# Moving small halo copies and two value loads from SyncE's queue to GpSimd's, in a convolution and gated-MLP gradient kernel

## The chip, the cores and the metric

The kernel runs on one core of a Trainium2 chip. The metric is the device time of one execution in microseconds, as the median of several runs. A core has five engines with a program each: TensorE (PE in the profile; its weight loads are PEld), VectorE (DVE), ScalarE (ACT), GpSimd (POOL) and SyncE (SP). Each works through its own program in order and waits on semaphores. A DMA transfer is started by an instruction of one of the engines; in this kernel SyncE and GpSimd start nearly all, and the page lists SyncE's as queue q1 (hardware_dynamic) and GpSimd's as q0 (software_dynamic). The transfers themselves run on the core's 16 DMA engines.

## The reference

The inputs are bfloat16, with S = 2048 rows, D = 512 columns and F = 1376. The forward function has two branches on the layer-normalised input `xn`:

```python
xn = layernorm(q)
# branch A: short convolution of k over 4 rows, product with v, long convolution
k_shift = sum(k_pad[:, t:t+S, :] * shift_k[:, 3 - t] for t in range(4))   # k_pad: 3 rows of zeros ahead
kv = k_shift * v
y  = irfft(rfft(pad(kv)) * rfft(pad(ssm_k)))[:S] + kv * ssm_D
s  = xn * y
# branch B: gated MLP
h  = sigmoid(xn @ w_gate) * (xn @ w_up)
out = q + s * silu(h @ w_down)
```

The kernel returns `out` and the gradients of a vector-Jacobian product with `grad_out`: of q, k, v, shift_k, ssm_k, ssm_D and of the three weight matrices. So it holds the forward long convolution, the MLP with its backward pass, the long convolution backward, and the short convolution backward. In the latter, `dks = dkv * v` and then `dk[row] = sum over lag 0..3 of dks[row + lag] * shift_k[lag]`.

## The kernel before

Rows are laid out as `row = 16 * partition + j`, so a partition holds 16 rows that follow each other. The 512 columns are treated in NG = 4 groups of GW = 128. A short convolution needs, beside the 16 rows of a partition, the three rows of its neighbour: the halo. In the forward stage a group of k is loaded with three extra rows in front:

```python
def ld_halo(eng, dst, src):
    eng.dma_start(dst[1:113], src[0:112])
    eng.dma_start(dst[113:128], src[112:127])

def ld_k(cp):
    c0, c1 = cp * GW, (cp + 1) * GW
    kh = kh_r.next()                                     # two buffers
    nc.gpsimd.memset(kh[0:1, 0:3, :], 0.0)
    nc.sync.dma_start(kh[:, 3:, :], kC[:, :, c0:c1])     # 16 rows, 512 KB
    ld_halo(nc.sync, kh[:, 0:3, :], kHalo[:, 0:3, c0:c1])   # 84 KB and 11.2 KB
    stA["kh", cp] = kh

def ld_v(cp):
    vg = vg_r.next()                                     # two buffers
    nc.sync.dma_start(vg, vC[:, :, cp * GW:(cp + 1) * GW])
    stA["vg", cp] = vg

def strV():                                              # VectorE part of branch A
    for cg in range(NG):
        # ... acc = short convolution of kh over four lags, 128x2048 each
        nc.gpsimd.dma_start(ksh_d[cg], acc.rearrange("p j d -> p (j d)"))   # shifted k, for the backward stage
        nc.vector.tensor_tensor(kvt, acc, vg, ALU.mult)
        if cg + 2 < NG:
            ld_k(cg + 2)
            ld_v(cg + 2)
        # ... first step of the transform of kvt
```

The K spectra of the same stage are stored with `nc.gpsimd.dma_start(KK_d[cg, qq, 0], KF)`, and their two halves are swapped by two copies of SyncE, `Ks[0:64] <- KF[64:128]` and `Ks[64:128] <- KF[0:64]`. The MLP's `h` is stored by GpSimd in `hF_d`.

In the backward stage, a group multiplies by the stored spectra `KK` (loaded by SyncE, three buffers), goes through the inverse steps `inv3` and `inv1` on TensorE with PSUM evictions on ScalarE or VectorE, and ends with the short convolution backward on VectorE:

```python
nc.vector.tensor_tensor(dks[:, 0:NJ, :], dkv, vg, ALU.mult)
nc.vector.memset(dks[96:P, NJ:NJ + 3, :], 0.0)
nc.sync.dma_start(dks[0:112, NJ:NJ + 3, :], dks[1:113, 0:3, :])      # halo from the next partition
nc.sync.dma_start(dks[112:127, NJ:NJ + 3, :], dks[113:128, 0:3, :])
nc.vector.tensor_tensor(dkv, dkv, ksh, ALU.mult)
# ... gradient of ssm_k: 32 matmuls, 2 evictions, 512 KB out
# ... gradient of shift_k: 64 matmuls of 32 columns (the diagonal), a product and a reduction on VectorE
for lag in range(4):
    src = dks[:, lag:lag + NJ, :]                        # lags 1 to 3 read the halo
    # lag 0: dk = src * skl;  lags 1 to 3: term = src * skl; dk = dk + term
# ... every second group: nc.sync.dma_start(o2C[...], dk)   (1 MB)
```

TensorE fills its time in this stage with the weight gradients `dW`: 35 blocks of 16 matmuls with 512 or 352 columns, each followed by an eviction and a store by SyncE. They depend on nothing in the backward convolution.

The order of instructions is not the order of this text. All operations are recorded first, with the regions that they read and write (the columns of a buffer, not its partitions, so the second halo copy of `dks` waits for the first). Then a list scheduler with a model of each engine, and of one pipe of transfers for GpSimd and one for the others, fixes the order of every engine, which engine does an eviction, and the PSUM banks:

```python
pipe = {"gpsimd": 0.0, "hw": 0.0}
# ...
if op.dma:
    occ, d = self.dcost(alt)
    me, other = ("gpsimd", "hw") if e == "gpsimd" else ("hw", "gpsimd")
    # ... start after this pipe's earlier transfers; fin = end of the transfer + a constant
```

All instructions are emitted from one line of the scheduler, L522, so the profile is read by operation and shape, not by line.

Of the kernel before, what the change touches and what calls it, by code (L numbers as in the profile page):

```python
# [23 lines left out]
NJ = 16  # L24
# [3 lines left out]
GW = D // NG  # L28
# [603 lines left out]
def cview(ap3):  # L632
    return ap3[0].rearrange("(p j) d -> p j d", j=NJ)
# [3 lines left out]
def kernel_impl(ctx, tc, A_q, A_k, A_v, A_shift_k, A_ssm_k, A_ssm_D, B_x, B_w_gate, B_w_up, B_w_down,  # L637
                grad_out, out_0, out_1, out_2, out_3, out_4, out_5, out_6, out_7, out_8, out_9):
    nc = tc.nc
    qC, kC, vC, goC = cview(A_q), cview(A_k), cview(A_v), cview(grad_out)  # L640
    o0C, o1C, o2C, o3C = cview(out_0), cview(out_1), cview(out_2), cview(out_3)
    kHalo = A_k[0][13:13 + 16 * 127].rearrange("(p j) d -> p j d", j=16)
# [15 lines left out]
    def ps_mm(shape, dt=f32, name=None):  # L658
        return nc.ps(PS["mm"], shape, dt)
# [142 lines left out]
# [5 lines that stand above are left out]
        c0, c1 = cp * GW, (cp + 1) * GW  # L807
        kh = kh_r.next()
        nc.gpsimd.memset(kh[0:1, 0:3, :], 0.0)
        nc.sync.dma_start(kh[:, 3:, :], kC[:, :, c0:c1])  # L810
        ld_halo(nc.sync, kh[:, 0:3, :], kHalo[:, 0:3, c0:c1])
        stA["kh", cp] = kh

    def ld_v(cp):
        vg = vg_r.next()
        nc.sync.dma_start(vg, vC[:, :, cp * GW:(cp + 1) * GW])
        stA["vg", cp] = vg

    skr_r = Ring(ar, [D * 4])
# [123 lines left out]
    def step3T(Qf, rows, qq, dst, sw):  # L943
        if rows:
            ps = ps_mm([64, 8, 2], name="ps_x")
            for h in range(2):
                src = Qf.rearrange("p (k g) -> p k g", g=64)[:, 32 * h:32 * h + 32, 16 * qq:16 * qq + 16]
                nc.tensor.matmul(ps[:, 32 * h:32 * h + 32].rearrange("p k g x -> p k (g x)"), BDq, src, start=True, stop=True)
            pv = ps.rearrange("p k g x -> p g k x")
            v = lambda a: a.rearrange("p (g k x) -> p g k x", g=8, x=2)  # L950
        else:
            pv = ps = ps_mm([1024], name="ps_x")
            for h in range(2):
                o = 1024 * qq + 512 * h
                nc.tensor.matmul(ps[:, h * 512:(h + 1) * 512], BDq, Qf[:, o:o + 512], start=True, stop=True)
            v = lambda a: a
        nc.evac(v(dst), pv[:], 1024)
        nc.scalar.copy(v(sw[0:64]), pv[64:128])
        nc.scalar.mul(v(sw[64:128]), pv[0:64], -1.0)
# [349 lines left out]
    def ld_KK(n):  # L1309
        if n < 16:  # L1310
            KK = KK_r.next()
            nc.sync.dma_start(KK, KK_d[n // 4, n % 4].rearrange("t p x -> p t x"))
            stC["KK", n] = KK
# [10 lines left out]
    def ld_bwd(cg):  # L1324
        c0, c1 = cg * GW, (cg + 1) * GW
        if cg % 2 == 0:
            stC["vg"] = vg_r.next()
            nc.sync.dma_start(stC["vg"], vC[:, :, c0:c0 + 256])
        ksh, kh = ksh_r.next(), kh_r.next()
        nc.sync.dma_start(ksh.rearrange("p j d -> p (j d)"), ksh_d[cg])  # L1330
        nc.gpsimd.memset(kh[0:1, 0:3, :], 0.0)
        nc.sync.dma_start(kh[:, 3:, :], kC[:, :, c0:c1])
        ld_halo(nc.sync, kh[:, 0:3, :], kHalo[:, 0:3, c0:c1])
        stC["bwd", cg] = (ksh, kh)

    def backC():
        for cg in range(NG):
            c0, c1 = cg * GW, (cg + 1) * GW
            B1, B2 = B1_r.next(), B2_r.next()
            ys = {}  # L1340
            for qq in range(5):
                if qq < 4:
                    n = cg * 4 + qq
                    while ("Qf", cg) not in stC:
                        yield 0
                    Xc, Xw = Xc_r.next(), Xw_r.next()
                    step3T(stC["Qf", cg], cg > 1, qq, Xc, Xw)
                    stC["nY"] = n + 1
                    yield 1024
                    KK = stC.pop(("KK", n))  # L1350
                    PP = P_r.next()
                    for t in range(2):
                        nc.vector.tensor_tensor(PP[:, t], Xc, KK[:, t], ALU.mult)
                        nc.vector.tensor_tensor(KK[:, t], Xw, KK[:, t], ALU.mult)
                    ys[qq] = (PP, KK)
                if qq == 2:
                    ld_bwd(cg)
                if qq > 0:
                    PP, KK = ys.pop(qq - 1)
                    inv3([(PP[:, 0], RC1), (KK[:, 0], RS2)], qq - 1, B1)  # L1360
                    yield 2048
                    inv3([(PP[:, 1], RC1), (KK[:, 1], RS2)], qq - 1, B2, True)
                    ld_KK(cg * 4 + qq + 2)
                    yield 2048
            dkv = y2A[:, :, c0:c1]
            yield from inv1(B1, dkv)
            ksh, kh = stC.pop(("bwd", cg))
            vg = stC["vg"][:, :, (cg % 2) * GW:(cg % 2 + 1) * GW]
            dks = dks_r.next()
            nc.vector.tensor_tensor(dks[:, 0:NJ, :], dkv, vg, ALU.mult)  # L1370
            nc.vector.memset(dks[96:P, NJ:NJ + 3, :], 0.0)
            nc.sync.dma_start(dks[0:112, NJ:NJ + 3, :], dks[1:113, 0:3, :])
            nc.sync.dma_start(dks[112:127, NJ:NJ + 3, :], dks[113:128, 0:3, :])
            nc.vector.tensor_tensor(dkv, dkv, ksh, ALU.mult)
            dKT = ar.view(B1_r.blks[0][0], [128, NJ], bf16)
            Bv = B2.rearrange("p j e g c -> p j (e g) c")
            for jh in range(2):
                pk = ps_mm([8, 128], name="ps_dk")
                for jj in range(8):
                    j = 8 * jh + jj  # L1380
                    for c in range(2):
                        nc.tensor.matmul(pk[:, jj, :], Bv[:, j, :, c], Ci[:, c, j, :], start=(c == 0), stop=(c == 1))
                nc.evac(dKT[:, :, 8 * jh:8 * jh + 8], pk[:].rearrange("p j n -> p n j"), 1024)
                yield 2048
            nc.sync.dma_start(out_5[c0:c1, :], dKT.rearrange("p n j -> p (n j)"))
            if cg % 2 == 1:
                nc.sync.dma_start(o3C[:, :, c0 - GW:c1], y2A[:, :, c0 - GW:c1])
            nc.vector.tensor_copy(dDo[:, cg:cg + 1], dKT[:, 0, 0:1])
            pa = ps_tr([4, 32], f32, name="ps_diag")
            for j in range(NJ):  # L1390
                for e in range(4):
                    es = slice(32 * e, 32 * e + 32)
                    nc.tensor.matmul(pa[es], dks[:, j, es], kh[:, j:j + 4, es], start=(j == 0), stop=(j == NJ - 1))
                if j == 7:
                    yield 2048
            nc.vector.tensor_tensor(dm, pa[:], id32[:, None, :].to_broadcast([P, 4, 32]), ALU.mult)
            nc.vector.tensor_reduce(res[:, cg, :], dm, AX.X, ALU.add)
            yield 2048
            if cg % 2 == 0:
                stC["dk"] = dk_r.next()  # L1400
            dk = stC["dk"][:, :, (cg % 2) * GW:(cg % 2 + 1) * GW]
            for lag in range(4):
                src = dks[:, lag:lag + NJ, :]
                skl = skb[:, lag:lag + 1, c0:c1].to_broadcast([P, NJ, GW])
                if lag == 0:
                    nc.vector.tensor_tensor(dk, src, skl, ALU.mult)
                else:
                    term = term_r.next()
                    nc.vector.tensor_tensor(term, src, skl, ALU.mult)
                    yield 512  # L1410
                    nc.vector.tensor_tensor(dk, dk, term, ALU.add)
                yield 512
            if cg % 2 == 1:
                nc.sync.dma_start(o2C[:, :, c0 - GW:c1], stC["dk"])
        for lag in range(4):
            nc.vector.tensor_copy(skout[:, :, lag:lag + 1], res[:, :, 3 - lag:4 - lag])
        po = ps_tr([GW, 4], f32)
        for t in range(4):
            nc.tensor.matmul(po[0:4, :, t], skout[:, :, t], ident, start=True, stop=True)
        nc.evac(row4[0:4, :], po[0:4].rearrange("p a t -> p (a t)"), 512)  # L1420
        nc.sync.dma_start(out_4.rearrange("(g p) t -> g (p t)", p=P), row4[0:4, :])
        pd = ps_tr([GW], f32)
        nc.tensor.matmul(pd[0:4, :], dDo, ident, start=True, stop=True)
        nc.evac(row6[0:4, :], pd[0:4], 128)
        nc.sync.dma_start(out_6.rearrange("(g p) -> g p", p=P), row6[0:4, :])
# [116 lines left out]
```

## Time and profile before

| What | us |
|---|---|
| time, median of 3 runs (520.12 to 521.19) | 520.15 |
| span of the profiled execution | 518.8 |
| TensorE busy | 490.4 |
| VectorE busy | 390.5 |
| ScalarE busy | 350.0 |
| GpSimd busy | 126.7 |

The page's second part cuts the span in 40 slices, each digit the busy tenths of one engine in one slice:

```profile
PE   4888899999999999999999999999999999999996
...
DVE  8799989775768799867689997427569588774844
ACT  7799989989874665565545456327869968676511
```

The first quarter is the forward convolution together with the first part of the MLP, the middle is the MLP forward and backward (to about 350 us), the last third is the backward convolution with the weight gradients beside it. The transfers concerned are these (columns: what moves where, the issuing engine's queue, the number, KB each, median us from issue to landing):

```profile
slab<-in_A_v_dram SPq DMA_DIRECT2D x4, 512.0 KB, 5.1
...
slab<-in_A_k_dram SPq DMA_DIRECT2D x8, 84.0 KB, 3.3
...
slab<-slab SPq DMA_DIRECT2D x4, 84.0 KB, 5.7
...
slab<-in_A_k_dram SPq DMA_DIRECT2D x8, 11.2 KB, 4.5
...
slab<-slab SPq DMA_DIRECT2D x4, 11.2 KB, 2.1
```

All on-chip buffers are one tile, named slab, so a copy inside it is `slab<-slab`: with 84 KB and 11.2 KB these are the halo copies of `dks`, with 128 KB the swaps of the K spectra.

### The profile page before, as it was taken

What the parts mean: (1) busy time and instruction counts of PE and PEld (TensorE: products, weight loads), DVE (VectorE), ACT (ScalarE), POOL (GpSimd) and SP (SyncE); (2) the same over time, 40 slices, a digit from 0 to 9 for tenths busy, and PEclk for the clock granted to TensorE, in tenths of its full rate; (3) what the DMA queues carried; (4) which work ended last, traced back from release to release, by engine and by line L of the source; (5) the groups of instructions that cost most, each with busy time, mean ns of one, the idle gap of its engine ahead of it and who ended that gap; (6) DMA issues with size and microseconds to landing.
All of it is one profiled execution on the core that took longest, in us unless ns stands there. A gap on an engine that the chain in (4) does not pass through costs nothing.

```text
span 518.8 us, 13496 instructions
## 1 busy us (share of the span) xinstructions
PE 490.4 (95%) x5382; PEld 350.5 (68%) x5437; DVE 390.5 (75%) x774; ACT 350.0 (67%) x465; POOL 126.7 (24%) x243
## 2 busy tenths in 40 slices
PE   4888899999999999999999999999999999999996
PEld 3778687889896776666665565545666756765653
DVE  8799989775768799867689997427569588774844
ACT  7799989989874665565545456327869968676511
POOL 7343435354514223514154310100000000000000
PEclk9999999999999999999999999999999999999999
DMA  9999987688998646727499947898899799999973
GB/s 211 307 277 281 297 251 247 218 274 206 270 214 203 190 118 177 194 94 198 113 249 248 274 136 186 218 269 227 194 277 178 219 261 189 270 224 221 200 213 113
DMA packets 181706, 112.93 MB, mean 218 GB/s; under 512 B 131434, under 2 KB 166154, under 8 KB 181387
## 3 DMA queue, kind: packets, MB, share of 16 engines
q1 hardware_dynamic: 170008, 78.17, 63.3%
q0 software_dynamic: 11104, 33.89, 20.1%
q8 instruction: 42, 0.69, 0.6%
q14 instruction: 22, 0.17, 0.1%
q10 hardware_dynamic: 530, 0.01, 0.1%
HBM read 37.65 MB, written 45.72 MB: 161 GB/s over the span
## 4 chain that ended last, share of the span: by engine, by line
PE 70%; ACT 12%; DVE 8%; DMA 4%; issue 3%; POOL 1%; SPq 0%; ACTq 0%; DVEq 0%; POOLq 0%
PE psum L522 70%; ACT slab L522 12%; DVE slab L522 8%; DMA out_dram<-slab 1%; DMA slab<-in_A_q_dram 1%; DMA slab<-in_A_ssm_D_dram 1%; POOL slab L522 1%; DMA slab<-KK_d 1%; SPq L522 0%; POOL hF_d L522 0%; ACTq L522 0%; DVEq L522 0%; POOLq L522 0%
## 5 line engine op out<-in xcount | busy, mean ns | idle before, releaser
L522 PE MATMUL psum<-slab 128*128 128x128 bf16 (+4 forms) x5382 | 490.4, 254 | 23.2 <-DVE slab L522 12.1
L522 PEld LDWEIGHTS <-slab 128*128 128x128 bf16 (+1 forms) x5437 | 350.5, 99 | 162.7 <-DVE slab L522 18.6
L522 DVE TENSOR_TENSOR slab<-slab 128x512 bf16<-128x512 bf16 (+7 forms) x488 | 267.8, 600 | 55.1 <-ACT slab L522 36.9
L522 ACT CAST slab<-psum 128x1024 bf16<-128x1024 f32 (+5 forms) x272 | 219.7, 852 | 93.3 <-PE psum L522 78.8
L522 ACT ACTIVATE slab<-psum 128x512 bf16<-128x512 f32 (+2 forms) x80 | 54.1, 679 | 37.0 <-PE psum L522 34.1
L522 ACT ACTIVATE slab<-slab 128x512 bf16<-128x512 bf16 (+3 forms) x71 | 56.8, 808 | 18.8 <-DVE slab L522 18.1
L522 ACT COPY slab<-psum 128x1024 bf16<-128x1024 bf16 (+1 forms) x40 | 37.3, 964 | 13.2 <-PE psum L522 13.2
L522 POOL DMA_DIRECT2D out_dram<-slab x32 | 17.5, 546 | 92.2 <-DVE slab L522 92.2
L522 DVE TENSOR_TENSOR slab<-psum,slab 128x512 bf16<-128x512 f32 (+2 forms) x47 | 29.4, 625 | 10.3 <-ACT slab L522 9.2
L522 DVE CAST slab<-psum 128x1024 bf16<-128x1024 f32 (+2 forms) x22 | 24.0, 1092 | 16.0 <-PE psum L522 13.6
L522 POOL MEMSET slab<- 1x384 bf16 (+2 forms) x13 | 4.8, 374 | 122.6 <-PE psum L522 118.1
L522 POOL DMA_DIRECT2D hF_d<-slab x48 | 26.1, 546 | 27.5 <-DVE slab L522 21.6
L522 DVE SCALAR_TENSOR_TENSOR slab<-psum,slab 128x512 bf16<-128x512 f32 x16 | 11.0, 688 | 27.8 <-PE psum L522 27.8
L522 POOL DMA_DIRECT2D KK_d<-slab x32 | 17.4, 544 | 22.8 <-ACT slab L522 20.7
L522 POOL DMA_DIRECT2D slab<-in_A_q_dram x29 | 16.0, 553 | 11.8 <-DMA out_dram<-slab 5.7
L522 DVE SCALAR_TENSOR_TENSOR slab<-slab 128x512 bf16<-128x512 bf16 (+3 forms) x41 | 17.1, 416 | 1.7 <-POOL slab L522 0.9
L522 POOL TENSOR_TENSOR slab<-slab 128x1 f32<-128x1 f32 x16 | 11.9, 745 | 18.2 <-DVE slab L522 18.0
L522 DVE STREAM_TRANSPOSE slab<-slab 128x1024 f32<-128x1024 f32 x8 | 14.3, 1827 | 2.7 <-ACT slab L522 2.7
L522 DVE TENSOR_SCALAR slab<-slab 128x1 f32<-128x1 f32 (+9 forms) x48 | 12.1, 267 | 4.2 <-POOL slab L522 3.3
L522 POOL DMA_DIRECT2D slab<-hF_d x18 | 9.6, 538 | 11.7 <-PE psum L522 10.6
L522 POOL DMA_DIRECT2D slab<-in_grad_out_dram x16 | 8.6, 540 | 9.9 <-DMA out_dram<-slab 9.0
L522 DVE COPY slab<-psum 128x1024 bf16<-128x1024 bf16 (+1 forms) x17 | 10.2, 621 | 1.1 <-PE psum L522 1.1
(20 smaller groups left out, 38.4 us busy)
## 6 DMA issues: line engine op xcount, KB each, us to landing
KK_d<-slab POOLq DMA_DIRECT2D x32, 256.0 KB, 4.7
slab<-KK_d SPq DMA_DIRECT2D x16, 512.0 KB, 4.7
slab<-in_A_k_dram SPq DMA_DIRECT2D x8, 512.0 KB, 7.4
hF_d<-slab POOLq DMA_DIRECT2D x32, 128.0 KB, 4.7
slab<-slab SPq DMA_DIRECT2D x32, 128.0 KB, 4.6
out_dram<-slab POOLq DMA_DIRECT2D x32, 128.0 KB, 3.3
uF_d<-slab SPq DMA_DIRECT2D x32, 128.0 KB, 2.6
gF_d<-slab SPq DMA_DIRECT2D x32, 128.0 KB, 2.7
```

Source lines behind the costliest of these rows:

```text
L522: getattr(getattr(self.nc, eng), meth)(*[place(v) for v in a], **{x: place(v) for x, v in k.items()})
```

## The change

In the forward stage, the halo rows of k and the whole of v for the third and fourth group of columns are issued by GpSimd; the first two groups, and the 16 rows of k of all groups, stay with SyncE. In the backward stage, both halo copies of `dks`, for all four groups, are issued by GpSimd; the loads of k and its halo there stay with SyncE. The aim is to take small transfers, and waits of SyncE on VectorE ahead of them, out of a queue in which many other transfers stand behind. Sizes, buffers and arithmetic stay as they are. As the scheduler has a pipe of its own for GpSimd's transfers, its model sees other end times, and the order of all engines differs from there on.

```diff
         kh = kh_r.next()
         nc.gpsimd.memset(kh[0:1, 0:3, :], 0.0)
+        q = nc.gpsimd if cp > 1 else nc.sync
         nc.sync.dma_start(kh[:, 3:, :], kC[:, :, c0:c1])
-        ld_halo(nc.sync, kh[:, 0:3, :], kHalo[:, 0:3, c0:c1])
+        ld_halo(q, kh[:, 0:3, :], kHalo[:, 0:3, c0:c1])
         stA["kh", cp] = kh
 
     def ld_v(cp):
         vg = vg_r.next()
-        nc.sync.dma_start(vg, vC[:, :, cp * GW:(cp + 1) * GW])
+        (nc.gpsimd if cp > 1 else nc.sync).dma_start(vg, vC[:, :, cp * GW:(cp + 1) * GW])
         stA["vg", cp] = vg
@@
             nc.vector.memset(dks[96:P, NJ:NJ + 3, :], 0.0)
-            nc.sync.dma_start(dks[0:112, NJ:NJ + 3, :], dks[1:113, 0:3, :])
-            nc.sync.dma_start(dks[112:127, NJ:NJ + 3, :], dks[113:128, 0:3, :])
+            nc.gpsimd.dma_start(dks[0:112, NJ:NJ + 3, :], dks[1:113, 0:3, :])
+            nc.gpsimd.dma_start(dks[112:127, NJ:NJ + 3, :], dks[113:128, 0:3, :])
```

## The prediction

> **What bounds the kernel now.** I read the page's busy shares first, then the windows by stage, then the waits, and last the two ends of the trace: the chain and the SyncE queue.
>
> ```profile
> PE 490.4 (95%) x5382; PEld 350.5 (68%) x5437; DVE 390.5 (75%) x774; ACT 350.0 (67%) x465; POOL 126.7 (24%) x243
> ...
> POOL 7343435354514223514154310100000000000000
> ```
>
> TensorE is busy for 490.4 of 518.8 us, so everything that any change of order could win is in the other 28.4 us. GpSimd, which gets the moved transfers, is half idle in the first quarter and has almost nothing to do in the last third. The windows say where the 28.4 us lie (columns: stretch, its length, busy time and count of PE, PEld, DVE, ACT, POOL, then clock, DMA share, GB/s):
>
> ```profile
> 0.00:40.00 40.00, 29.05 (x360) 25.00 (x363) 34.50 (x84) 32.89 (x44) 20.28 (x45) 1.00 0.98 269
> 40.00:80.00 40.00, 36.09 (x557) 32.22 (x559) 37.66 (x50) 37.44 (x45) 15.74 (x28) 1.00 0.89 271
> 80.00:120.00 40.00, 37.91 (x580) 33.81 (x584) 33.67 (x53) 36.64 (x44) 18.75 (x33) 1.00 0.79 246
> ...
> 382.70:417.80 35.10, 34.34 (x363) 22.73 (x368) 27.33 (x36) 29.92 (x33) 0.41 (x1) 1.00 0.83 220
> 417.80:457.30 39.50, 38.47 (x395) 25.32 (x397) 31.36 (x40) 28.66 (x32) 0.41 (x1) 1.00 1.01 246
> 457.30:496.10 38.80, 37.14 (x377) 23.69 (x382) 25.86 (x35) 24.24 (x28) 0.00 (x0) 1.00 1.06 220
> 496.10:518.80 22.70, 17.47 (x102) 9.54 (x100) 8.20 (x12) 4.14 (x8) 0.00 (x0) 0.97 0.48 147
> ```
>
> Three places: the forward convolution (0 to 120 us: 10.95 + 3.91 + 2.09 = 16.95 us idle, with VectorE and ScalarE near full), the backward convolution (the three rows from 382.7 to 496.1 are cut where VectorE reduces the diagonal of one group, so each is one group's length: 0.76 + 1.03 + 1.66 = 3.45 us idle), and the drain after the last matmul at 513.6 (5.2 us). The middle, 120 to 360 us, has TensorE at over 99%, and the change touches nothing there but the order of instructions.
>
> In the list of waits, just one belongs to the moved copies; the SyncE queue and VectorE around it, and the chain's end, are:
>
> ```profile
> DVE slab L522 <- DMA slab<-slab: 6.9, 1, 6.9
> ```
>
> ```profile
> 493.66 1.22 DVE L522 TENSOR_TENSOR slab<-slab 128x2048 bf16<-128x2048 bf16 x1
> ...
> 494.77 0.98 SPq L522 DMA_DIRECT2D slab<-slab  x1
> ...
> 495.85 5.83 SPq L522 DMA_DIRECT2D out_dram<-slab  x4
> ...
> 501.74 0.88 SPq L522 DMA_DIRECT2D slab<-slab  x1
> ...
> 503.88 7.51 DVE L522 TENSOR_TENSOR slab<-slab 128x2048 bf16<-128x2048 bf16 x6 [6.86 <-DMA slab<-slab]
> ...
> 512.15 3.16 SPq L522 DMA_DIRECT2D out_dram<-slab  x2
> ```
>
> ```profile
> 496.86 16.74 PE psum L522 x98
> 513.67 0.45 ACT slab L522
> ```
>
> The first halo copy of the last group leaves at 494.77, the second only at 501.74, after four output transfers in the same queue; VectorE waits for it until 503.88. But the chain of the end is not VectorE: it is 16.74 us of weight-gradient matmuls and one eviction. VectorE's wait reaches the end only through its result, a 1 MB store, of which more below.
>
> [...]the share of the DMA engines is 0.79 to 1.06 in the stages concerned[...]the trace has 5.1 us for the first copy at 494.77 (in SyncE's queue) and 2.1 us for the 11 KB one[...]the trace has GpSimd's issues at 538 to 553 ns in every group[...].
>
> **The change part by part.** *Forward loads.* Six transfers (two V loads of 512 KB, two halo pairs of 84 and 11 KB) go from SyncE to GpSimd. On GpSimd that is 6 x 0.54 = 3.2 us more[...], on an engine busy for 54.8 of the first 120 us. Are they in time? SyncE issues V of the third group at 39.4 and it lands in 5.1 us; it is used after the third write of the shifted k, which GpSimd issues at 68.35. That leaves some 24 us of slack. In the changed order of GpSimd the V load stands right after an hF store that before left at 36.7 and the second halo piece directly behind it, so both land by about 43, and the third group's convolution does not begin before the second one's result goes out at 51.5. For the fourth group the second halo piece stands after two KK stores (57 to 59 in before), lands by about 63, needed at 68. So no new wait, and none removed: in before no engine waits for a k or V load. What remains is the shuffle: the list scheduler that orders this kernel has other ends of transfers to work with, and every engine's order differs from some 28 us on. By counting in the two programs' orders, VectorE loses six PSUM evictions in all and ScalarE gets them; about three of these lie in this stage. SyncE is freed of some 4 us of issuing while it also feeds the half-swaps of the K spectra. I give this stage -1.6 us of its 6.7 us of TensorE idle between 28 and 100 us, with a spread of 3 either way; it is a guess from the size of the idle time, not a count.
>
> *Backward halo copies.* Eight issues go (SyncE spends 1.61 + 0.95 + 0.62 + 3.96 + 0.60 + 0.91 + 0.98 + 0.88 = 10.5 us on them), eight of 0.54 us come on an idle GpSimd. In the first three groups VectorE never waits for them, so nothing is won directly. In the last: product done at 494.9, issue 0.5, landing about 3, issue 0.5, landing 2.1, so VectorE goes on at about 501 instead of 503.9.
>
> *The drain.* In before the 1 MB store of dk is issued at 512.15 behind VectorE's end at 511.4 and fills the DMA engines at about 290 GB/s until 517.0; the last two 88 KB stores share that. In the changed order of SyncE this store stands before the last 128x512 block and the four 128x352 blocks, so it is gone before TensorE ends. Then the last eviction at 514.1 is followed by a small store alone: its bytes are out by about 515.6 instead of 517.0. That is -1.4 us.
>
> *The fill of the backward stage.* TensorE's order in the two programs shows the largest shift. After the last small transposing matmul there were 30 matmuls of 128x512 and 64 of 128x352; now 71 and 64. So 41 x 0.237 us (233.4 us by 985) = 9.7 us of weight-gradient work leaves the groups and is done in the tail, alone. TensorE's work by group (0.237, 0.166 and 0.153 us for 512, 352 and 256 columns) becomes 34.34 + 14 x 0.237 + 4 x 0.153 = 38.3, then 38.47 - 13 x 0.237 - 20 x 0.166 - 4 x 0.153 = 31.5, then 37.14 - 41 x 0.237 + 20 x 0.166 = 30.7 us. VectorE's instructions in the three groups, each by its own mean (686 ns for 128x1024, 1221 for 128x2048), are now 27.2, 29.7 and 26.0 us. So in the second group VectorE would be busy for 94% of TensorE's time. In the forward stage, by the windows of 8 us from 28 to 100 us, VectorE is busy for 66.4, ScalarE for 68.9 and TensorE for 65.3 of 72 us: with VectorE at 92%, TensorE was idle for 9%. I take 2.5 and 2.0 us of idle for the second and third group, 0.8 for the first: 5.3 against 3.45, that is +1.9 us.
>
> Sum: 520.15 - 1.6 - 1.4 + 1.9 = 519.05, so 519.0 us.
>
> **The rivals.** (a) *A clear gain, 513 to 516.* If the backward groups do run at TensorE's pace, as the new order supposes, the +1.9 becomes -1, and if the forward stage loses half its idle time that is -3. For it: groups of 35.1 us with 0.76 us idle did happen in before. Against: the copies themselves were not waited for in the groups. (b) *Slower, 522 to 526.* With less filler between them, the backward matmuls wait for evictions and for KK loads (VectorE waits 5.4 us for these in before), and each wait now falls on an empty TensorE. For it: 94% on VectorE. Against: KK loads no longer stand behind halo copies in SyncE's queue. (c) *No change, 520.* Everything moved was hidden, the freed VectorE time is slack, and the shuffles cancel. (d) *GpSimd becomes the late one:* it issues in order, and a V load behind a waiting KK store (5.9 us the longest such wait) comes late; the slack of 24 us speaks against.
>
> **Range and chances.** The spreads of 3 us (forward), 3 us (backward) and 0.7 us (drain) are independent: about 4.3 us in all for 8 in 10, so 514.5 to 523.5. 2% is 10.4 us. Faster by that would need more than a third of all idle time to go; slower needs both stages to turn bad. So 0.03 faster, 0.94 same, 0.03 slower.
>
> **What would show it.** Right: TensorE still about 490 us busy; VectorE's wait for the halo copy shorter than 4.5 us or gone; the dk store over before the last matmul and the span ending about 3.5 us after it instead of 5.2; the tail of weight-gradient matmuls after the last group some 27 us long; TensorE idle of 2 us or more in the second or third backward group. Wrong: a VectorE wait on a V or k load before 100 us (then d), or idle time from 0 to 120 us that moves by more than 4 us (then my guess of the shuffle is mis-sized), or TensorE's busy sum itself changing by several us.

## The result and the profile after

| | before | after |
|---|---|---|
| time, median of 4 runs each, us | 520.67 (520.12 to 522.37) | 517.74 (517.25 to 518.21) |
| ratio | | 0.9938 [0.9911, 0.9965] |
| span of the profiled execution, us | 518.8 | 516.4 |
| TensorE idle, 0 to 160 us | 17.2 | 19.8 |
| TensorE idle in the second to fourth backward group | 3.45 | 1.75 |
| from the last matmul to the end | 5.2 | 3.1 |

The kernel is 2.9 us faster, and 519.0 us were predicted, from the 520.15 of the first three runs of before. The page of after gives these busy sums and slices of GpSimd:

```profile
PE 489.1 (95%) x5379; PEld 350.0 (68%) x5437; DVE 387.6 (75%) x768; ACT 353.2 (68%) x471; POOL 136.7 (26%) x257
...
POOL 7255634444413432424153511000010010010000
```

TensorE's sum is the same within 1.3 us: no work went away. GpSimd has 14 instructions more. One caution goes with all idle times of this first pair of profiles: some matmul records are missing from both. Before's page counts 5382 matmuls and after's 5379, against 5437 weight loads, and the page of every later run has 5437 of each. Time of a missing matmul looks like idle time, so these figures are too large (in the three backward groups 3.45 and 1.75 here, 1.86 and 0.80 in the second pair further down). The windows, with the columns as in the prediction (stretch, length, busy time and count of PE, PEld, DVE, ACT, POOL, clock, DMA share, GB/s), cut again where VectorE reduces a group's diagonal:

```profile
0.00:40.00 40.00, 28.31 (x355) 24.12 (x358) 34.21 (x84) 32.54 (x44) 21.49 (x45) 1.00 0.95 264
40.00:80.00 40.00, 37.31 (x580) 33.89 (x585) 37.28 (x53) 39.99 (x49) 19.40 (x35) 1.00 0.92 299
80.00:120.00 40.00, 37.64 (x588) 34.19 (x590) 33.58 (x50) 36.41 (x44) 17.36 (x33) 1.00 0.77 230
...
120.00:160.00 40.00, 36.90 (x558) 32.86 (x562) 24.20 (x47) 31.22 (x44) 15.19 (x30) 1.00 1.10 201
...
384.50:422.90 38.40, 37.98 (x381) 24.69 (x386) 30.15 (x36) 32.81 (x37) 1.49 (x3) 1.00 0.95 235
422.90:455.30 32.40, 31.85 (x359) 21.79 (x361) 27.21 (x36) 26.72 (x30) 1.49 (x3) 1.00 1.06 270
455.30:487.40 32.10, 31.32 (x355) 21.32 (x358) 24.48 (x33) 23.59 (x28) 1.07 (x2) 1.00 1.05 219
```

Of the parts that the prediction named, the groups and the end are better: the backward groups end 8.7 us earlier (487.40 instead of 496.10) with the weight-gradient work moved behind them, and TensorE is idle in them for 0.42 + 0.55 + 0.78 us. From 0 to 120 us nothing changed (16.7 us idle against 17.0), but from 120 to 160 us, where before had 0.3 us, there are now 3.1.

The last group's halo in the list of waits, then in the timeline (start, length, engine, operation; in brackets the idle time ahead and what ended it), and the end of the chain:

```profile
DVE slab L522 <- DMA slab<-slab: 1.3, 1, 1.3
```

```profile
483.27 3.62 DVE L522 TENSOR_TENSOR slab<-slab 128x2048 bf16<-128x2048 bf16 x3 [5.25 <-ACT slab L522]
...
484.79 1.07 POOL L522 DMA_DIRECT2D slab<-slab  x2 [30.24 <-DVE slab L522]
...
489.22 7.52 DVE L522 TENSOR_TENSOR slab<-slab 128x2048 bf16<-128x2048 bf16 x6 [1.33 <-DMA slab<-slab]
```

```profile
486.22 10.85 PE psum L522 x50
497.12 16.20 PE psum L522 x94
513.39 0.45 ACT slab L522
```

The product of `dks`, the first of the three at 483.27, is done at 484.5. GpSimd issues both copies at once, two in 1.07 us, and VectorE goes on at 489.22, 4.7 us after the product. In before it was 10.6 us. There the product is the last of the operations ahead of the memset of the halo rows:

```profile
481.94 11.38 DVE L522 TENSOR_TENSOR slab<-slab 128x1024 bf16<-128x1024 bf16 x11 [1.80 <-DMA slab<-KK_d]
493.41 0.22 DVE L522 MEMSET slab<- 32x192 uint32 x1
```

It is done at 493.3, and the prediction's line at 493.66 is already the next product, `dkv * ksh`. (In the queue-only kernel below, which keeps before's order, GpSimd issues both copies 0.3 us after that memset, while the operation behind it still runs.) The first copy of before thus waited for SyncE until 494.77, and the second until 501.74. TensorE runs from 486.22 to 513.3 almost only on weight gradients, and an eviction ends the chain as before.

Once issued, the pair is no quicker from GpSimd: from issue to landing the 84 KB copies take 4.0 us and the 11.2 KB ones 4.8 us in after (medians of four). From SyncE it is 5.7 and 2.1 us in before. What GpSimd wins is the time until the copies leave: in the last group both are issued within 1.4 us of the product, while in before the second begins only 8.4 us after it.

### The profile page after: what moved, and what is told of

Same layout as the page of the kernel before. It is cut to its first block, busy times and chain, and to the rows that moved or that the text cites. A ratio compares the mean times of both kernels' runs of the same rounds, so it can differ in the third digit from the quotient of the medians.

```text
span 516.4 us, 13503 instructions
## 1 busy us (share of the span) xinstructions
PE 489.1 (95%) x5379; PEld 350.0 (68%) x5437; DVE 387.6 (75%) x768; ACT 353.2 (68%) x471; POOL 136.7 (26%) x257
## 4 chain that ended last, share of the span: by engine, by line
PE 77%; ACT 9%; DVE 7%; issue 4%; DMA 2%; POOL 1%; ACTq 0%; DVEq 0%; POOLq 0%
PE psum L522 77%; ACT slab L522 9%; DVE slab L522 7%; DMA slab<-in_A_q_dram 1%; DMA slab<-in_A_ssm_D_dram 1%; POOL slab L522 1%; POOL hF_d L522 0%; ACTq L522 0%; DVEq L522 0%; POOLq L522 0%
## 5 line engine op out<-in xcount | busy, mean ns | idle before, releaser
L522 PE MATMUL psum<-slab 128*128 128x128 bf16 (+4 forms) x5379 | 489.1, 254 | 24.2 <-ACT slab L522 10.1
L522 PEld LDWEIGHTS <-slab 128*128 128x128 bf16 (+1 forms) x5437 | 350.0, 99 | 163.0 <-issue 15.8
L522 DVE TENSOR_TENSOR slab<-slab 128x512 bf16<-128x512 bf16 (+6 forms) x488 | 268.9, 601 | 53.1 <-ACT slab L522 45.8
L522 ACT CAST slab<-psum 128x1024 bf16<-128x1024 f32 (+5 forms) x276 | 224.5, 867 | 91.1 <-PE psum L522 81.4
L522 ACT ACTIVATE slab<-psum 128x512 bf16<-128x512 f32 (+2 forms) x80 | 55.2, 694 | 38.9 <-PE psum L522 35.6
L522 ACT ACTIVATE slab<-slab 128x512 bf16<-128x512 bf16 (+3 forms) x71 | 56.8, 810 | 15.2 <-DVE slab L522 13.9
L522 ACT COPY slab<-psum 128x1024 bf16<-128x1024 bf16 (+1 forms) x42 | 39.2, 987 | 13.5 <-PE psum L522 13.5
L522 POOL DMA_DIRECT2D out_dram<-slab x32 | 17.4, 545 | 95.4 <-DVE slab L522 95.4
L522 POOL DMA_DIRECT2D slab<-slab x8 | 4.3, 544 | 130.9 <-DVE slab L522 130.6
L522 DVE TENSOR_TENSOR slab<-psum,slab 128x512 bf16<-128x512 f32 (+2 forms) x47 | 29.4, 627 | 10.6 <-ACT slab L522 7.7
L522 POOL DMA_DIRECT2D hF_d<-slab x48 | 26.2, 547 | 30.7 <-DVE slab L522 30.0
L522 DVE SCALAR_TENSOR_TENSOR slab<-psum,slab 128x512 bf16<-128x512 f32 x16 | 11.1, 691 | 27.1 <-PE psum L522 27.1
L522 DVE CAST slab<-psum 128x1024 bf16<-128x1024 f32 (+1 forms) x18 | 20.2, 1131 | 4.1 <-PE psum L522 4.0
L522 POOL DMA_DIRECT2D KK_d<-slab x32 | 17.4, 546 | 17.0 <-ACT slab L522 15.5
L522 POOL DMA_DIRECT2D slab<-in_A_q_dram x29 | 16.1, 556 | 11.0 <-DVE slab L522 4.8
L522 DVE SCALAR_TENSOR_TENSOR slab<-slab 128x512 bf16<-128x512 bf16 (+3 forms) x41 | 17.1, 416 | 0.8
L522 DVE STREAM_TRANSPOSE slab<-slab 128x1024 f32<-128x1024 f32 x8 | 14.3, 1834 | 4.0 <-ACT slab L522 4.0
L522 DVE TENSOR_SCALAR slab<-slab 128x1 f32<-128x1 f32 (+9 forms) x48 | 12.1, 268 | 6.3 <-POOL slab L522 5.4
L522 POOL TENSOR_TENSOR slab<-slab 128x1 f32<-128x1 f32 x16 | 9.8, 615 | 14.0 <-DVE slab L522 13.8
L522 POOL DMA_DIRECT2D slab<-hF_d x18 | 9.7, 541 | 12.2 <-PE psum L522 10.1
L522 DVE BATCH_NORM_STATS2 slab<-slab 128x6 f32<-128x512 bf16 x16 | 10.9, 686 | 0.5 <-DMA slab<-in_A_q_dram 0.5
L522 POOL DMA_DIRECT2D slab<-in_grad_out_dram x16 | 8.6, 540 | 7.6 <-DMA out_dram<-slab 7.1
```

What stands on the lines that cost most here:

```text
L522: getattr(getattr(self.nc, eng), meth)(*[place(v) for v in a], **{x: place(v) for x, v in k.items()})
```

## Experiments

Theory T1: the gain is the backward order, made with prompt halo copies, plus the earlier dk store; the forward half is worth little. Rival T2: the queue alone brings the gain, in whatever order. Rival T3: the gain is the order alone, a lucky draw of the list scheduler, and who issues does not matter. The three are put as the runs came to separate them; each run's own theory stands in its text. An edit can shift the scheduler's line, so L522 is L524 to L527 in some runs. Each run is compared with before on the same chip; the ratios carry 95% intervals.

**Only the queue, and only the order.** In the first kernel before's order of every engine is kept, and the eight `dks` copies are emitted on GpSimd. In the second, after's order is kept, and all 14 moved transfers are emitted on SyncE.

```diff
# only the queue (before), where the finished order is emitted
+                eng = op.mark or eng      # "gpsimd" for the eight dks copies
# only the order (after)
+                eng = op.mark or eng      # "sync" for the six loads and eight copies
```

> The kernel before with every engine's order kept, and only the eight halo copies of dks taken from SyncE's program into GpSimd's. Theory (the gain is the drain: the 1 MB store of dk leaves early enough to be off the DMA engines when the last weight-gradient block is stored): VectorE's wait in the last group falls from 6.9 to 1 to 2.5 us, the dk store is issued at about 510 instead of 512.15, TensorE ends as before, and the time falls by 1.3 to 1.9 us, ratio about 0.997. Rival 1 (SyncE's queue is relieved all through the backward stage, so KK loads come earlier and TensorE idles less): the three group intervals lose 1.5 us or more of idle, ratio 0.994 as for the whole change. Rival 2 (only the new order counts): nothing, ratio 1.000.

> The changed kernel with every engine's order kept, and all fourteen moved transfers issued by SyncE again, each at the place in time that the order gives it. Theory (drain, through the order: the dk store stands before the last five stores in SyncE's program whoever issues the halo): the store still leaves some 13 us before TensorE's end, the drain stays near 3.1 us, and the time is that of the changed kernel within 1 us, ratio 0.994 to 0.996. Rival 1 (SyncE's relief): the gain goes, ratio 0.998 or more, with group intervals that idle by 3 us or more again, as in the kernel before (3.45).

Measured: the queue alone 518.38 us, 0.9985 [0.9976, 0.9994]; the order alone 542.58 us, 1.0458 [1.0435, 1.0481]. The second is the largest miss of the study: I took the order for the source of the gain, and with the copies back in SyncE's queue it costs 24 us. Its windows by group, and around the gap of the second group; then its SyncE queue and VectorE at the start of the first of these groups, and TensorE's gap in the second:

```profile
383.13:428.07 44.94, 40.38 (x385) 26.03 (x384) 30.01 (x34) 32.44 (x37) 0.41 (x1) 0.92 0.77 197
428.07:468.90 40.83, 34.10 (x362) 22.76 (x361) 27.29 (x35) 26.68 (x30) 0.41 (x1) 0.92 0.84 220
468.90:511.72 42.82, 35.19 (x360) 23.79 (x358) 24.62 (x32) 23.56 (x28) 0.00 (x0) 0.88 0.91 184
...
440.00:450.00 10.00, 4.21 (x40) 2.47 (x37) 7.93 (x7) 6.57 (x8) 0.00 (x0) 0.88 0.33 96
450.00:460.00 10.00, 9.42 (x77) 6.52 (x78) 6.96 (x12) 3.65 (x5) 0.00 (x0) 0.78 0.89 244
```

```profile
382.39 0.61 SPq L524 DMA_DIRECT2D slab<-slab  x1
...
385.47 5.72 SPq L524 DMA_DIRECT2D out_dram<-slab  x1
391.24 0.95 SPq L524 DMA_DIRECT2D slab<-slab  x1
...
393.87 12.97 DVE L524 TENSOR_TENSOR slab<-slab 128x2048 bf16<-128x2048 bf16 x14 [6.52 <-DMA slab<-slab]
...
450.07 0.29 PE L524 MATMUL psum<-slab 128*128 128x128 bf16 x1 [5.86 <-DVE slab L524]
```

The first halo copy leaves at 382.39; the second stands behind an output store that holds the queue for 5.72 us, leaves at 391.24, and VectorE goes on only at 393.87, after 6.5 us of waiting. In the next two groups VectorE waits 7.1 and 10.1 us, which the profile puts down to an output store and to a load of spectra; the second copy leaves late there too (its issue begins at 436.06 and 478.15, some 10 and 4 us after the first). In after VectorE has no wait for a halo in this group. TensorE is idle for 4.6, 6.7 and 7.6 us in the three groups, and it also works more slowly: their 1107 matmuls are busy for 109.67 us, where the same 1107 take 101.76 us in the second profile of after. The granted clock is 0.92, 0.92 and 0.88 in these groups, with a gap of TensorE in each (4.5, 5.9 and 5.7 us), and 0.78 in the 10 us from the end of the 5.86 us gap; in the groups of before and after, where no gap is over 0.7 us, it is 1.00. Whether the gaps themselves lower the clock was not tried. So T3 falls: the order is worth nothing without prompt copies. T2 falls in part: in before's order, prompt copies win 0.8 us (0.15%) of the 2.9.

**Does the second copy's place alone do it?** After's order, `dks` copies on SyncE, but the second directly behind the first; the forward loads stay on GpSimd.

```diff
# where the finished order is emitted (after); x holds each second copy under its first
+ seq = [t for s in seq if not isinstance(s[0].mark, Op) for t in ([s, x[id(s[0])]] if id(s[0]) in x else [s])]
# ...
+                eng = "sync" if op.mark else eng
```

> The changed kernel with every engine's order kept, forward loads on GpSimd as changed, and only the eight halo copies of dks issued by SyncE again, the second of each pair directly behind the first (when the changed order was run with all moved transfers on SyncE, at 1.046, the second copy stood up to three transfers behind the first, one of them waiting 4 to 6 us for its own condition). Theory (what costs 24 us there is the place of the second copy behind a transfer that waits, not SyncE's queue as such): VectorE's waits for halo and KK fall from some 31 us to under 10, TensorE's idle in the groups to under 4 us, ratio 0.996 to 1.003. Rival (SyncE's queue itself, with transposes and megabyte stores in it, brings the copies too late for this order): the groups idle by 8 us or more, ratio 1.015 or more.

Measured: 522.10 us against 520.74, 1.0034 [1.0017, 1.0052], slightly above what T1 gave. Most of the 24 us are recovered. The forward loads, which differ too, cost nothing that shows: up to 160 us TensorE is idle for 16.7 us with them on SyncE and for 16.3 with them on GpSimd. So the second copy's place was most of the harm. The rest is in the third of the groups (SyncE, VectorE; then the window):

```profile
457.94 3.34 SPq L526 DMA_TRANSPOSE slab<-uF_d  x1
461.38 1.57 SPq L526 DMA_DIRECT2D slab<-slab  x2
...
464.24 10.25 DVE L526 TENSOR_TENSOR slab<-slab 128x2048 bf16<-128x2048 bf16 x10 [3.92 <-DMA slab<-slab]
```

```profile
454.38:490.76 36.38, 33.16 (x360) 22.62 (x358) 24.63 (x32) 23.66 (x28) 0.00 (x0) 0.95 0.98 209
```

The pair is issued behind a transposing load that holds the queue for 3.34 us, VectorE waits 3.92 us, and the group takes 36.4 us with 3.2 us of TensorE idle, against 32.2 with 0.4 in the second profile of after. One gap of 3.1 us goes with a clock of 0.95 here, and the same 360 matmuls are busy for 33.16 us against 31.76. Given this order, GpSimd's queue is therefore worth 0.65 to 0.96% (3.4 to 5 us) beyond a close pair on SyncE (1.0034 here, 0.9969 and 0.9938 for after). What counts is the place in a program that runs in order: with the copies on SyncE the ratio is 1.0458 with the second one behind other transfers and 1.0034 with it behind the first. The use of the DMA engines differs little: their share in that group is 0.98 (209 GB/s) here and 1.05 (219 GB/s) in after.

**The two halves of the change.** In one kernel only the `dks` copies go to GpSimd, in the other only the forward loads.

```diff
# backward half only (against before), both copies
-            nc.sync.dma_start(dks[...], dks[...])
+            nc.gpsimd.dma_start(dks[...], dks[...])
# forward half only (against after), both copies
-            nc.gpsimd.dma_start(dks[...], dks[...])
+            nc.sync.dma_start(dks[...], dks[...])
```

> The second half of the change alone: halo copies of dks by GpSimd, forward loads all by SyncE, order made anew by the scheduler. Theory (the change's forward half cost 2.6 us of TensorE idle up to 160 us, its backward half gave 1.7 us in the groups and 2.1 us in the drain): forward idle as before (about 17.2 us up to 160 us), backward and drain as in the changed kernel, so some 2 to 3 us faster than the changed kernel, ratio to before 0.988 to 0.991. Rival (the order of each stage is a lottery, not a property of the moved transfers): forward as before since nothing there differs, but a backward stage that can land anywhere between 1.5 and 5 us of idle, ratio 0.990 to 1.000.

> The first half of the change alone: halo of k and V of the third and fourth group by GpSimd, halo copies of dks by SyncE, order made anew. Theory: forward idle as in the changed kernel (about 19.8 us up to 160 us, 2.6 us more than before), backward and drain much as before, so slower than before by 2 to 3 us, ratio 1.004 to 1.006. Rival (the forward half is what gives the gain, for instance through the state in which it hands over to the backward stage): ratio below 0.998.

Measured on one chip, before at 520.10: the backward half 517.21, 0.9949 [0.9936, 0.9962]; the forward half 519.94, 1.0002 [0.9983, 1.0021]. The backward half carries the gain, though less than the 0.988 to 0.991 I gave it. For the forward half I expected a loss of 2 to 3 us from the new idle time behind 120 us. The comparison shows none beyond its interval of 1 us either way. The profiles of all kernels sort into two sets by the forward order. With before's (before twice and six variants) TensorE has done 1489 to 1507 matmuls by 120 us, with 15.9 us idle in the mean, and is idle for 0.3 us in the mean from 120 to 160. With after's (after twice and four variants) it has done 1518 to 1537, with 15.3 us idle, and is then idle for 2.0. The order lets TensorE run ahead, and then it waits, between 136 and 144 us, for evictions on ScalarE (1.16 and 1.05 us in after). The two together are a loss of some 1 us, small enough to hide in the interval. The one with the loads on SyncE is in this set too (1537 matmuls; 1.4 us), so it is the order and not the queue. One profile stands out: that of the backward half, with before's order, is idle for 1.6 us from 120 to 160, after VectorE waited 2.2 us for a load of `grad_out`; it is of an execution of 520.2 us, where the median was 517.2.

**The drain.** Three kernels attack it. In before, the last dk store (1 MB) is left out, so the right half of the gradient of k is not written; or, in before, the second halo copy is put right behind the first on SyncE, so that VectorE's chain and its store come earlier; or, in after, the dk store is held back until the third of the last four 352-column blocks is stored.

```diff
# no last store (before); "last" marks the o2C store of the last group
+                if op.mark == "last":
+                    continue
# adjacent (before); x holds each second dks copy under its first
+ seq = [t for s in seq if s[0].mark is None for t in ([s, x[id(s[0])]] if id(s[0]) in x else [s])]
# late store (after); x is the marked store, put ahead of SyncE's last instruction
+ at = [i for i, s in enumerate(seq) if s[0].alts[0][0] == "sync"][-1]
+ seq[at:at] = x
```

> The kernel before without the last 1 MB store of dk (the right half of the gradient of k is not written); nothing else differs. Theory (drain): the time from TensorE's last matmul to the end falls from 5.2 to about 3.1 us, all else equal, so 1.8 to 2.2 us less, ratio 0.996. Rival (the end is fixed cost of the last small store and the store of dk is hidden beside it): nothing, ratio 1.000.

> The kernel before, halo copies on SyncE as before, but the second copy of each group directly behind the first in SyncE's program instead of one to five transfers later. Theory (the wait of 6.9 us was the place of the second copy in the program, not the queue): VectorE's wait in the last group falls to 2 to 3.5 us, the dk store is issued at about 510, and the time falls as with the copies on GpSimd, by 1.3 to 1.9 us, ratio about 0.997. Rival (a copy in SyncE's queue stands behind the megabyte store of the same queue whatever its place): the wait stays over 5 us and the ratio is 1.000.

> The changed kernel with one difference: the last 1 MB store of dk is held back in SyncE's program until the third of the four 128x352 blocks is stored, as late as the kernel before had it. Theory (drain): its bytes run until some 3.5 us after TensorE's last matmul, the drain grows from 3.1 to about 4.8 us, and the time rises by 1.3 to 2 us against the changed kernel, ratio to before 0.997 to 0.998. Rival: no difference from the changed kernel, ratio 0.994.

Measured: no last store 517.90 us, 0.9985 [0.9975, 0.9995], drain 3.3 us; adjacent 518.30 us, 0.9985 [0.9977, 0.9994], drain 3.2 us; late store 520.05 us, 1.0007 [0.9994, 1.0021], drain 5.2 us. In the end of the late-store kernel (same columns as the windows above; the last two numbers are DMA share and GB/s) the store fills the DMA engines after TensorE has stopped:

```profile
513.00:514.00 1.00, 0.10 (x1) 0.00 (x0) 0.00 (x0) 0.45 (x1) 0.00 (x0) 1.00 1.03 293
...
515.00:516.00 1.00, 0.00 (x0) 0.00 (x0) 0.00 (x0) 0.00 (x0) 0.00 (x0) 1.00 1.02 289
516.00:517.00 1.00, 0.00 (x0) 0.00 (x0) 0.00 (x0) 0.00 (x0) 0.00 (x0) 1.00 0.89 257
```

All three move the drain in the direction named. Taking the store away, bringing it forward by a close pair, and bringing it forward with GpSimd (the queue alone, above: drain 3.3) are worth the same 0.8 us in before (by their ratios), so in before's order an early halo copy pays through the drain and through nothing else that shows. I had expected 1.3 to 2 us; the profile of before that I read had a drain of 5.2, two later ones of the old end had 4.5 and 4.1, so the 2 us were taken from a long one. Holding the store back costs 2.8 us against the backward half on the same chip, 0.7 more than the 2.1 us by which the drain grew. But the late store was added to after, which was not run on that chip; against after's ratios of 0.9938 and 0.9969 elsewhere it costs 3.6 or 2.0 us, so the rest is within what these comparisons differ by.

**Both kernels again, on one chip.**

> The kernel before, unchanged, for a second profile and as a gauge of how far two sets of runs of one program differ. Theory (the drain of 5.2 us in the first profile was at the long end, as the dk store left at 512.15 only because VectorE waited 6.9 us for the halo): ratio 1.000 with an interval of about 0.001, drain between 4 and 5.2 us, 2.3 to 3.5 us of idle in the three group intervals. Rival (the drain is always 5.2 us, so that leaving out the store should have given 2 us and not 0.8): drain 5.1 us or more.

> The changed kernel, unchanged, with more runs and on the same chip as its neighbours. Theory (the backward half gives the whole gain, about half a per cent, and the forward half nothing): ratio 0.994 to 0.996, group intervals idle for 0.8 to 1.9 us, drain 3.1 us. Rival (the forward half costs or gives 2 us): ratio over 0.997 or under 0.992, away from the 0.995 of the backward half alone.

Measured, before at 519.54: before again 519.34, 1.0003 [0.9989, 1.0016]; after again 517.95, 0.9969 [0.9953, 0.9986]. So the gain is 1.6 us here and 2.9 in the first comparison. This pair of profiles is the fairest to read, as both are of one chip and have all 5437 matmuls. Groups and end, before:

```profile
383.79:418.37 34.58, 34.49 (x368) 22.65 (x366) 27.13 (x35) 29.05 (x33) 0.41 (x1) 1.00 0.83 218
418.37:457.83 39.46, 38.59 (x399) 25.40 (x398) 31.33 (x38) 29.22 (x32) 0.41 (x1) 1.00 1.05 248
457.83:495.64 37.81, 36.91 (x379) 23.32 (x378) 25.79 (x33) 23.68 (x28) 0.00 (x0) 1.00 1.03 225
...
514.00:515.00 1.00, 0.00 (x0) 0.00 (x0) 0.00 (x0) 0.00 (x0) 0.00 (x0) 1.00 1.04 291
515.00:516.00 1.00, 0.00 (x0) 0.00 (x0) 0.00 (x0) 0.00 (x0) 0.00 (x0) 1.00 0.80 235
```

and after:

```profile
383.95:421.97 38.02, 38.00 (x385) 24.54 (x384) 29.95 (x34) 32.43 (x37) 1.49 (x3) 1.00 0.96 231
421.97:454.34 32.37, 32.00 (x362) 21.78 (x361) 27.20 (x35) 26.69 (x30) 1.49 (x3) 1.00 1.06 270
454.34:486.51 32.17, 31.76 (x360) 21.33 (x358) 24.55 (x32) 23.66 (x28) 1.07 (x2) 1.00 1.04 219
...
514.00:515.00 1.00, 0.00 (x0) 0.00 (x0) 0.00 (x0) 0.00 (x0) 0.00 (x0) 1.00 0.07 20
```

Idle in the groups 1.86 against 0.80 us, the drain 4.5 against 3.15, and up to 160 us 15.9 against 16.1: -1.1, -1.4 and +0.2, of a span that is 2.1 us shorter. At 514 us before still moves 291 GB/s, after 20. The waits of before in these groups that after does not have at all are:

```profile
DVE slab L522 <- DMA slab<-KK_d: 5.0, 2, 3.9
...
ACT slab L522 <- DMA out_dram<-slab: 2.6, 1, 2.6
...
DVE slab L522 <- DMA out_dram<-slab: 1.7, 1, 1.7
```

In after VectorE does the sums of the short convolution soon after the product instead of keeping them for later, and meets the spectra when they have landed. That these waits go with the order, and not with a relieved SyncE queue, is seen in the queue-only kernel, which has before's order, the copies on GpSimd, and still this wait:

```profile
DVE slab L524 <- DMA slab<-KK_d: 4.5, 2, 3.3
```

That the earlier sums are what saves the 1.1 us is not shown: no run moves the sums alone, and the kernels of the next part do them early in some or all groups, keep such waits (5.8 us) or lose them, and idle more in either case.

**The scheduler's model.** In before the scheduler takes the second `dks` copy to depend on the first, since it compares columns only. In the last two kernels this false dependency is removed and everything is ordered anew, once with the copies on SyncE, once on GpSimd. The second was meant as the best candidate: true dependencies and a free queue.

```diff
-nc.sync.dma_start(dks[0:112, ...])      # and the second
+h1 = nc.sync.dma_start(dks[0:112, ...]) # or nc.gpsimd
+h2 = nc.sync.dma_start(dks[112:127, ...])
+h2.deps.discard(h1.n)
```

> The kernel before with the halo copies on SyncE, but the scheduler is told that the second copy doesn't depend on the first (they touch other partitions of the same columns), and makes the order anew; the two copies now stand directly behind each other. Theory (the new order, with the sums of dk early on VectorE, comes from a model that sees the halo early; GpSimd's queue isn't needed for it): the dk store stands before the last five stores, VectorE's waits for the halo stay under 3 us, ratio 0.995 to 0.997. Rival (copies in SyncE's program come late whatever the model thinks, as when the changed order was run with them on SyncE): VectorE waits of 5 us or more for halo or KK, groups that idle by 4 us or more, ratio 1.002 or more.

> The backward half alone (halo copies of dks on GpSimd, forward loads on SyncE), and the scheduler is told that the second copy doesn't depend on the first; order made anew. It is the candidate for a version faster than both. Theory: the halo is on time already with the backward half alone (VectorE waits 0.8 us), so the model's truth adds little: ratio 0.993 to 0.996. Rival (an earlier halo in the model lets the sums of dk start earlier still and shortens the groups): ratio 0.992 or less.

Measured, same chip as the pair above: on SyncE 517.91, 0.9974 [0.9960, 0.9987]; on GpSimd 521.56, 1.0041 [1.0027, 1.0056]. On SyncE the waits for the halo did not stay under 3 us: in the last group a close pair leaves only at 493.08, behind three transposing loads and a store, and VectorE waits 6.2 us. Its drain is 3.2 us all the same. The candidate is slower than before, and the kernel with no GpSimd copy is as fast as after. The one on GpSimd differs from the backward half only in that dependency, and by 0.9% in time. In its three groups TensorE is idle for 4.7 us, against 1.9 there (in the long execution named above), and VectorE waits longer for evictions:

```profile
DVE slab L522 <- ACT slab L522: 23.5, 9, 6.0
```

in this kernel, and in the backward half:

```profile
DVE slab L522 <- ACT slab L522: 17.1, 9, 6.0
```

Which of these evictions costs TensorE its time was not tried. So the order that the list scheduler happens to draw is worth as much as the change itself, in either direction. No run was clearly faster than after; the backward half alone (0.9949) equals it within the intervals.

## Why the prediction was right or wrong

The time, 517.74 us, lay in the range and 1.3 us under the middle. By the steps:

- *Backward fill, +1.9: wrong in its sign, and this is the step that failed.* I took 5.3 us of idle time in the three groups, against 3.45; there were 1.75, and in the repeat 0.80 against 1.86. The repeat has all matmuls, so the term was -1.1, and the 3.45 from which I started was already 1.6 us too large for want of 12 matmul records or more in these windows (363, 395 and 377 matmuls beside 368, 397 and 382 weight loads). The shift of TensorE's work was counted right (38.3, 31.5 and 30.7 predicted; 37.98, 31.85 and 31.32 measured), and so was the tail of some 27 us (27.1). VectorE's sum was near too (82.9 predicted, 81.8 measured), but not its split: 30.2, 27.2 and 24.5 instead of 27.2, 29.7 and 26.0. The long first group took 3 us of what I had put on the second and third, and the second came to 84% instead of 94%. And the step went from a share of 94% to idle time as if VectorE's waits stayed; but those for the spectra and the output buffers went away: VectorE spent 6.7 us on them in before's repeat and none in after's. This was rival (a)'s -1, whose working stood in the prediction.
- *Forward, -1.6: the guess was mis-sized; it is 0 within 1 us.* The forward half by itself measured 1.0002. Something of the kind did happen (0.6 us less idle up to 120 us in the mean of the profiles), and more than that was given back between 120 and 160 us (1.7 us), a stretch that I had called untouched but for the order. That the window of the prediction ended at 120 hid the return.
- *Drain, -1.4: right in mechanism and, by the profiles of one chip, in size.* In time, the three kernels that shorten it in before's order (queue only, no last store, adjacent) gave 0.8 us. After's drain was 3.1 where 3.5 was predicted.
- *Halo of the last group: right in direction, wrong in its parts.* VectorE goes on 4.7 us after the product, not 6.1. I let the second copy wait for the first, as the scheduler's model does, but GpSimd issues the two in 1.07 us. I also took the next product for that of `dks` and so put before's delay at 9.0 us, where it was 10.6, and I took 2.1 us for the landing of the 11.2 KB copy from SyncE, where from GpSimd it took 3.8 us in this group. The landing of the 84 KB copy, for which I had set about 3 us as an estimate, took 4.1 there. As predicted it does not reach the end except through the store.
- *GpSimd (rival d):* no engine waited on a V or k load before 100 us except GpSimd itself (2.5 us once in the repeat). Rival (b), waits on an empty TensorE, did not come in this kernel, but describes the order on SyncE (1.0458), with the halo in the place of the evictions.

With -1.1 for the groups, -0.8 to -1.4 for the drain and 0 within 1 us for the forward stage, the sum is -1.9 to -2.5, within 1 us; the comparisons of the whole gave -1.6 and -2.9. So the prediction came near the time in part by luck: it set a gain of 1.6 us in the forward stage that did not come against a loss of 1.9 us in the groups that did not come either.

## What to carry to other kernels

In a program that runs in order, ask of every small transfer what stands ahead of it and what that waits for: here, in one and the same order, the same two copies of a group cost nothing from GpSimd, 3 to 5 us over the kernel as a close pair on SyncE, and over 20 us with other transfers between them. A list scheduler builds its order on the times it believes in, so a change of queue is two changes, and each half has to be run by itself with the order held. Here a single dependency in its model moved the time by 0.9%, so a gain of half a per cent is within the luck of such a scheduler; and idle time must be followed past the end of the stage that wins, since what TensorE gains early it may wait for later.

## What the runs showed of the hardware that was not expected

In the last group GpSimd issues the 84 KB and the 11 KB copy in 1.07 us together in after and in 1.05 in the queue-only kernel, without waiting between them. There, from the product to the resumption of VectorE, the pair takes 4.7 and 4.9 us from GpSimd in after's two profiles and 6.2 in before's order (queue only). From SyncE it takes 6.0 as a close pair in before's order, 6.8 as one in after's, and 10.3 to 10.6 with four stores between. So in before's order a close pair on SyncE is as quick as one on GpSimd (6.0 us against 6.2). And TensorE lost time twice in the order run on SyncE: beside 18.9 us of idle time in the three groups, their matmuls were busy for 7.9 us more than the same ones in after's second profile, at a granted clock of 0.88 to 0.92 over whole groups. Even after's order with a close pair, with one gap of 3.1 us, had 0.95 in its third group and 1.4 us more of busy time.
